# Sliding-window attention and a gated feed-forward: attention issued between the feed-forward's matmuls, with two-head block-diagonal score products and tanh for sigmoid

## The chip, the cores and the metric

The kernel runs on one core of a Trainium2 chip. The metric is the device time of one execution in microseconds (us), the median of several runs.

The core has five engines, each with its own list of instructions; the instructions of VectorE, ScalarE and GpSimd start in the order in which the kernel issues them. The engines are TensorE (PE in the profile; PEld are its weight loads, which overlap its products), VectorE (DVE), ScalarE (ACT), GpSimd (POOL) and the sync engine (SP), which here only issues transfers. "Granted clock" or PEclk is the share of TensorE's full clock that the throttle let through.

## The reference

There are 8 batches, 8 heads, 576 positions and 64 dimensions per head. Each query sees itself and the 63 positions before it. The result, laid out as 4608 tokens of 512 values, goes through a gated feed-forward with 1536 hidden values. The reference, shortened:

```python
scores = scale * np.matmul(q, k.transpose(0, 1, 3, 2))          # scale = 1/8
mask = (rel >= 0) & (rel < 64)                                  # rel = query position - key position
scores = np.where(mask, scores, -1e9)
attn = softmax(scores)                                          # written out in the original
x = (attn @ v).transpose(0, 2, 1, 3).reshape(4608, 512)
g = x @ w_gate                                                  # 512 x 1536
out = (g * (1.0 / (1.0 + np.exp(-g))) * (x @ w_val)) @ w_out    # w_out: 1536 x 512
```

## The kernel before

It works in two stages. The first goes through all 64 heads. A head's q and k are cast, transposed on TensorE, and multiplied in blocks of 64 queries by 128 keys.

```python
        for b in range(B):
            for h in range(H):
                po = (h % 2) * 64
                kc = h // 2
                qbh = q[b, h]
                kbh = k[b, h]
                vbh = v[b, h]
                # ... tiles and loads of q, k, v and of v shifted by 64 rows, on two queues ...
                q_bf = nat.tile([P, 5, D], BF16, name="q_bf", tag="q_bf")
                k_bf = nat.tile([P, 5, D], BF16, name="k_bf", tag="k_bf")
                nc.vector.tensor_copy(q_bf[:, 0:4, :], q_nat[:, 0:4, :])
                nc.vector.tensor_copy(q_bf[0:64, 4, :], q_nat[0:64, 4, :])
                nc.vector.tensor_copy(k_bf[:, 0:4, :], k_nat[:, 0:4, :])
                nc.vector.tensor_copy(k_bf[0:64, 4, :], k_nat[0:64, 4, :])
                qT = tp_pool.tile([64, S], BF16, name="qT", tag="qT")
                kT = tp_pool.tile([64, S], BF16, name="kT", tag="kT")
                tpq = psB.tile([64, 640], BF16, name="tpq", tag="tpq")
                tpk = psB.tile([64, 640], BF16, name="tpk", tag="tpk")
                for c in range(4):
                    nc.tensor.transpose(tpq[:, 128 * c:128 * c + 128], q_bf[:, c, :], identb[:])
                    nc.tensor.transpose(tpk[:, 128 * c:128 * c + 128], k_bf[:, c, :], identb[:])
                nc.tensor.transpose(tpq[:, 512:576], q_bf[0:64, 4, :], identb[0:64, 0:64])
                nc.tensor.transpose(tpk[:, 512:576], k_bf[0:64, 4, :], identb[0:64, 0:64])
                nc.scalar.copy(qT[:, :], tpq[:, 0:576])
                nc.vector.tensor_copy(kT[:, :], tpk[:, 0:576])
                # ... casts of v and of the shifted v, with a column of ones beside each ...
                groups = [list(range(8)), [8]]
                for gi, blocks in enumerate(groups):
                    nb = len(blocks)
                    mask_t = mask_first if (gi == 0) else mask_reg
                    S_ps = psA.tile([P, 8, 64], FP32, name="S_ps", tag="S_ps")
                    for mu, i in enumerate(blocks):
                        k0 = 0 if i == 0 else 64 * (i - 1)
                        nc.tensor.matmul(
                            S_ps[:, mu, :],
                            kT[:, k0:k0 + 128],
                            qT[:, 64 * i:64 * i + 64],
                        )
                    E = grp.tile([P, 8, 64], BF16, name="E", tag="E")
                    nc.scalar.activation(
                        E[:, 0:nb, :], S_ps[:, 0:nb, :], AF.Exp, bias=0.0, scale=SCALE
                    )
                    nc.vector.tensor_mul(E[:, 0:nb, :], E[:, 0:nb, :], mask_t[:, 0:nb, :])

                    ntiles = 2 if nb == 8 else 1
                    OU = []
                    for tt in range(ntiles):
                        OU.append(psA.tile([64, 4, 65], FP32, name="OU", tag="OU"))
                    for mu, i in enumerate(blocks):
                        tt = mu // 4
                        jj = mu % 4
                        if i == 0:
                            vv = v_aug[:, 0, :]
                        elif i % 2 == 1:
                            vv = v_aug[:, (i - 1) // 2, :]
                        else:
                            vv = vs_aug[:, (i - 2) // 2, :]
                        nc.tensor.matmul(OU[tt][:, jj, :], E[:, mu, :], vv)
                    R = grp.tile([64, 8], FP32, name="R", tag="R")
                    for tt in range(ntiles):
                        nbt = min(4, nb - 4 * tt)
                        nc.vector.reciprocal(R[:, 4 * tt:4 * tt + nbt], OU[tt][:, 0:nbt, 64])
                    Dm = grp.tile([64, 8, 64], BF16, name="Dm", tag="Dm")
                    nc.vector.tensor_mul(
                        Dm[:, 0:nb, :],
                        ident8[:, 0:nb, :],
                        R[:, 0:nb].to_broadcast((64, nb, 64)),
                    )
                    OU_sb = grp.tile([64, 8, 64], BF16, name="OU_sb", tag="OU_sb")
                    for tt in range(ntiles):
                        nbt = min(4, nb - 4 * tt)
                        nc.vector.tensor_copy(
                            OU_sb[:, 4 * tt:4 * tt + nbt, :], OU[tt][:, 0:nbt, 0:64]
                        )
                    XT = psA.tile([P, 8, 64], FP32, name="XT", tag="XT")
                    for mu, i in enumerate(blocks):
                        nc.tensor.matmul(
                            XT[po:po + 64, mu, :],
                            OU_sb[:, mu, :],
                            Dm[:, mu, :],
                        )
                    # ... copied into xT by ScalarE ...
```

The second stage goes through nine tiles of 512 tokens. `fps` has two PSUM banks for each of `g_ps` and `v_ps`, `fops` has one for `o_ps`.

```python
            hT = fsb.tile([P, 12, 512], BF16, name="hT", tag="hT")
            for m in range(12):
                g_ps = fps.tile([P, 512], FP32, name="g_ps", tag="g_ps")
                v_ps = fps.tile([P, 512], FP32, name="v_ps", tag="v_ps")
                for kk in range(4):
                    nc.tensor.matmul(
                        g_ps[:], wg[:, kk, 128 * m:128 * m + 128],
                        xT[:, kk, tok0:tok0 + 512],
                        start=(kk == 0), stop=(kk == 3),
                    )
                for kk in range(4):
                    nc.tensor.matmul(
                        v_ps[:], wv[:, kk, 128 * m:128 * m + 128],
                        xT[:, kk, tok0:tok0 + 512],
                        start=(kk == 0), stop=(kk == 3),
                    )
                sg = fsb.tile([P, 512], BF16, name="sg", tag="sg")
                nc.scalar.activation(sg[:], g_ps[:], AF.Sigmoid)
                tq = fsb.tile([P, 512], BF16, name="tq", tag="tq")
                nc.vector.tensor_mul(tq[:], sg[:], g_ps[:])
                nc.vector.tensor_mul(hT[:, m, :], tq[:], v_ps[:])
            for sub in range(4):
                o_ps = fops.tile([P, 512], FP32, name="o_ps", tag="o_ps")
                for kk in range(12):
                    nc.tensor.matmul(
                        o_ps[:],
                        hT[:, kk, 128 * sub:128 * sub + 128],
                        wo[:, kk, :],
                        start=(kk == 0), stop=(kk == 11),
                    )
                os_ = ostage.tile([P, 512], FP32, name="os_", tag="os_")
                nc.scalar.copy(os_[:], o_ps[:])
                nc.sync.dma_start(out[tok0 + 128 * sub:tok0 + 128 * sub + 128, :], os_[:])
```

The softmax here doesn't subtract the row's maximum and nothing guards it: scores larger than these inputs give would overflow.

## Time and profile before

| | |
|---|---|
| time | 605.42 us, median of 3 runs (604.98 to 605.86) |
| start: loads of weights, TensorE idle | 23 us |
| attention | 23 to about 315 us, about 4.5 us per head |
| feed-forward | 315 us to the end, 31.1 us per tile |

The top of the profile's page gives the span, each engine's busy time with its share and number of instructions, and then the span in 40 equal slices of 15 us, where a digit is the busy share of a slice in tenths.

```profile
span 602.7 us, 10344 instructions
...
PE 517.5 (86%) x3638; PEld 306.0 (51%) x3664; DVE 406.2 (67%) x1439; ACT 218.1 (36%) x466; POOL 3.9 (1%) x12
...
PE   0068888888888888888869999999999999999996
...
DVE  1578898898989889898966455554546463637270
...
```

Counted from 1, VectorE is at 8 or 9 tenths in slices 4 to 20 and TensorE is at 9 in slices 22 to 39. The two stages have two different limits, and the average shares (86% and 67%) describe neither. The view by windows shows it for one stretch inside each stage. Its columns are the window, its length, then busy time and number of instructions for PE, PEld, DVE, ACT and POOL, the granted clock, the DMA share and GB/s.

```profile
...
40.00:300.00 260.00, 220.29 (x2208) 166.44 (x2205) 229.52 (x1130) 121.96 (x300) 0.00 (x0) 1.00 0.57 128
320.00:590.00 270.00, 268.02 (x1224) 121.83 (x1248) 147.49 (x215) 82.77 (x140) 0.00 (x0) 1.00 0.09 32
...
```

TensorE's 220 us of "busy" time in the first window says little: its many small products are drawn overlapping (nine score products of one group span 0.66 us at 121.58 us, while the mean of one is 237 ns). The feed-forward can be read better from distances: equal projections of two tiles lie 31.08 us apart (341.11 to 372.19 us), and a tile has 144 matmuls, so one takes 0.216 us. Nine tiles need at least 280 us of TensorE. The chain that ended last says the same. It is followed back from the last instruction, and its shares are of the whole span.

```profile
...
PE 46%; ACT 0%; issue 0%; ACTq 0%
PE v_ps L221 16%; PE g_ps L215 15%; PE o_ps L234 15%; ACT os__8291 L241 0%; ACT os__8323 L241 0%; ACT os__8307 L241 0%; ACT os__8339 L241 0%; ACTq L241 0%
...
```

The costliest groups of instructions are shown with busy time, the mean time of one in ns, and the idle time before them with what ended it.

```profile
...
L229 DVE TENSOR_TENSOR tq<-sg,g_ps 128x512 bf16<-128x512 bf16 x108 | 74.2, 687 | 81.5 <-ACT sg L227 81.5
L215 PE MATMUL g_ps<-xT,wg 128*128 128x512 bf16 x422 | 110.2, 381 | 1.4 <-ACT xT L196 0.7
...
L234 PE MATMUL o_ps<-wo,hT 128*128 128x512 bf16 x424 | 98.5, 379 | 2.4 <-ACT os__8291 L241 0.7
...
L184 DVE CAST OU_sb<-OU 64x256 bf16<-64x256 f32 (+1 forms) x192 | 63.1, 329 | 0.0
...
```

The groups with shapes kept apart: first come two kinds of weight loads, then the reciprocal at two sizes.

```profile
...
L215 PEld LDWEIGHTS <-wg 128*128 128x128 bf16 x432 | 42.3, 98 | 52.0 <-issue 1.5
...
L126 PEld LDWEIGHTS <-k_bf 128*64 128x64 bf16 x256 | 27.4, 163 | 33.0 <-DVE k_bf L118 29.3 <-issue 0.9
...
L174 DVE RECIPROCAL R<-OU 64x4 f32<-64x4 f32 x128 | 22.1, 173 | 9.2 <-PE OU L170 1.7
...
L174 DVE RECIPROCAL R<-OU 64x1 f32<-64x1 f32 x64 | 9.7, 151 | 2.0
...
```

A weight load of 128 rows and 128 columns takes 98 ns and one of 128 rows and 64 columns 163 ns. The Trainium skill, page "TensorE: Matmul & The Clock Gate", section "Weight-path perf modes", says that the fast weight load is on when there are 128 weights of a type other than FP32; this trace agrees. The reciprocal of one element per partition takes 151 ns and of four 173 ns: the slope is about 7 ns per element.

### The profile page before, as it was taken

How to read it: one execution, taken by the hardware profiler on the slowest of the kernel's cores; microseconds unless marked ns; L12 is line 12 of the kernel's file. 1: busy time of each engine (PE TensorE's matmuls, PEld its weight loads, DVE VectorE, ACT ScalarE, POOL GpSimd, SP SyncE). 2: the span in 40 equal slices, each digit the busy share in tenths (PEclk: the TensorE clock that was granted, in tenths of full speed). 3: DMA queues.
4: the chain of work that ended last, by engine and by line, in shares of the span. 5: the costliest groups of instructions: out<-in, count | busy, mean ns of one | idle time of the engine just before them, and what ended most of it. 6: DMA issues, size and time to landing. Idle time of an engine off the chain costs nothing. (4 is left out here: it accounts for less than half of the span.)

```text
span 602.7 us, 10344 instructions
## 1 busy us (share of the span) xinstructions
PE 517.5 (86%) x3638; PEld 306.0 (51%) x3664; DVE 406.2 (67%) x1439; ACT 218.1 (36%) x466; POOL 3.9 (1%) x12
## 2 busy tenths in 40 slices
PE   0068888888888888888869999999999999999996
PEld 0046666666666666666654444444444444444442
DVE  1578898898989889898966455554546463637270
ACT  0044444444444444444434232333233232323331
POOL 2000000000000000000000000000000000000000
PEclk9999999999999999999999999999999999999999
DMA  8955565555656555665510000101010101010101
GB/s 345 344 125 118 124 140 130 125 122 132 136 117 139 131 129 119 136 138 117 130 28 1 35 36 29 41 18 53 18 52 18 52 4 67 2 71 0 71 0 70
DMA packets 153251, 55.20 MB, mean 92 GB/s; under 512 B 146032, under 2 KB 146032, under 8 KB 153200
## 3 DMA queue, kind: packets, MB, share of 16 engines
q1 hardware_dynamic: 79968, 33.57, 20.2%
q10 hardware_dynamic: 73232, 20.98, 14.5%
q8 instruction: 28, 0.46, 0.3%
q14 instruction: 23, 0.19, 0.1%
HBM read 45.09 MB, written 9.44 MB: 90 GB/s over the span
## 5 line engine op out<-in xcount | busy, mean ns | idle before, releaser
L229 DVE TENSOR_TENSOR tq<-sg,g_ps 128x512 bf16<-128x512 bf16 x108 | 74.2, 687 | 81.5 <-ACT sg L227 81.5
L215 PE MATMUL g_ps<-xT,wg 128*128 128x512 bf16 x422 | 110.2, 381 | 1.4 <-ACT xT L196 0.7
L221 PE MATMUL v_ps<-xT,wv 128*128 128x512 bf16 x424 | 110.5, 381 | 0.5
L230 DVE TENSOR_TENSOR hT<-tq,v_ps 128x512 bf16<-128x512 bf16 x108 | 74.1, 687 | 43.6 <-PE v_ps L221 34.2
L227 ACT ACTIVATE sg<-g_ps 128x512 bf16<-128x512 f32 x108 | 64.5, 597 | 106.2 <-PE g_ps L215 101.4
L234 PE MATMUL o_ps<-wo,hT 128*128 128x512 bf16 x424 | 98.5, 379 | 2.4 <-ACT os__8291 L241 0.7
L152 ACT ACTIVATE E<-S_ps 128x512 bf16<-128x512 f32 (+1 forms) x128 | 46.7, 408 | 76.9 <-PE S_ps L146 61.3
L234 PEld LDWEIGHTS <-hT 128*128 128x128 bf16 x432 | 42.2, 98 | 53.5 <-issue 2.9
L215 PEld LDWEIGHTS <-wg 128*128 128x128 bf16 x432 | 42.3, 98 | 52.0 <-issue 1.5
L221 PEld LDWEIGHTS <-wv 128*128 128x128 bf16 x432 | 42.4, 98 | 51.7 <-issue 1.1
L189 PE MATMUL XT<-Dm,OU_sb 64*64 64x64 bf16 x576 | 55.1, 240 | 14.5 <-DVE Dm L176 14.4
L126 PE MATMUL tpk<-identb,k_bf 128*64 128x128 bf16 x256 | 41.4, 313 | 30.2 <-DVE k_bf L118 25.5
L184 DVE CAST OU_sb<-OU 64x256 bf16<-64x256 f32 (+1 forms) x192 | 63.1, 329 | 0.0
L196 ACT CAST xT<-XT 64x512 bf16<-64x512 f32 (+1 forms) x128 | 44.1, 393 | 48.2 <-PE XT L189 46.9
L170 PEld LDWEIGHTS <-E 128*64 128x64 bf16 x576 | 41.0, 151 | 30.8 <-DVE E L155 23.1
L176 DVE TENSOR_TENSOR Dm<-ident_76,R 64x512 bf16<-64x512 bf16 (+1 forms) x128 | 56.2, 439 | 0.0
L170 PE MATMUL OU<-v_aug,E 128*64 128x65 bf16 x320 | 41.5, 248 | 15.1 <-DVE E L155 12.6
L189 PEld LDWEIGHTS <-OU_sb 64*64 64x64 bf16 x576 | 41.7, 144 | 24.5 <-DVE Dm L176 15.9
L146 PE MATMUL S_ps<-qT,kT 64*128 64x64 bf16 x576 | 42.4, 237 | 12.7 <-DVE kT L130 10.9
L129 ACT COPY qT<-tpq 64x576 bf16<-64x576 bf16 x64 | 40.3, 630 | 28.1 <-PE tpq L127 21.1
L170 PE MATMUL OU<-vs_aug,E 128*64 128x65 bf16 x256 | 46.6, 249 | 0.7 <-DVE OU_sb L184 0.6
L125 PE MATMUL tpq<-identb,q_bf 128*64 128x128 bf16 x256 | 41.9, 311 | 4.1 <-DVE q_bf L116 2.8
(76 smaller groups left out, 375.5 us busy)
## 6 DMA issues: line engine op xcount, KB each, us to landing
k_nat<-in_k_dram ACTq DMA_DIRECT2D x64, 128.0 KB, 2.8
vs_nat<-in_v_dram ACTq DMA_DIRECT2D x64, 128.0 KB, 2.6
q_nat<-in_q_dram SPq DMA_DIRECT2D x64, 128.0 KB, 2.6
v_nat<-in_v_dram SPq DMA_DIRECT2D x64, 128.0 KB, 2.8
wv_f<-in_moe_w_val_dram ACTq DMA_DIRECT2D x1, 3072.0 KB, 18.0
wg_f<-in_moe_w_gate_dram SPq DMA_DIRECT2D x1, 3072.0 KB, 17.0
wo_f<-in_moe_w_out_dram SPq DMA_DIRECT2D x1, 3072.0 KB, 27.2
k_nat<-in_k_dram ACTq DMA_DIRECT2D x64, 16.0 KB, 2.5
```

The lines of the kernel that those rows point to most:

```text
L152: nc.scalar.activation(E[:, 0:nb, :], S_ps[:, 0:nb, :], AF.Exp, bias=0.0, scale=SCALE)
L170: nc.tensor.matmul(OU[tt][:, jj, :], E[:, mu, :], vv)
L176: nc.vector.tensor_mul(Dm[:, 0:nb, :], ident8[:, 0:nb, :], R[:, 0:nb].to_broadcast((64, nb, 64)),)
L184: nc.vector.tensor_copy(OU_sb[:, 4 * tt:4 * tt + nbt, :], OU[tt][:, 0:nbt, 0:64])
L189: nc.tensor.matmul(XT[po:po + 64, mu, :], OU_sb[:, mu, :], Dm[:, mu, :],)
L196: nc.scalar.copy(xT[po:po + 64, kc, t0:t0 + 64 * nb], XT[po:po + 64, 0:nb, :],)
L215: nc.tensor.matmul(g_ps[:], wg[:, kk, 128 * m:128 * m + 128], xT[:, kk, tok0:tok0 + 512], start=(kk == 0), stop=(kk == 3),)
L221: nc.tensor.matmul(v_ps[:], wv[:, kk, 128 * m:128 * m + 128], xT[:, kk, tok0:tok0 + 512], start=(kk == 0), stop=(kk == 3),)
L227: nc.scalar.activation(sg[:], g_ps[:], AF.Sigmoid)
L229: nc.vector.tensor_mul(tq[:], sg[:], g_ps[:])
L230: nc.vector.tensor_mul(hT[:, m, :], tq[:], v_ps[:])
L234: nc.tensor.matmul(o_ps[:], hT[:, kk, 128 * sub:128 * sub + 128], wo[:, kk, :], start=(kk == 0), stop=(kk == 11),)
```

## The change

The intent is to keep TensorE on the feed-forward while the other engines prepare the attention of later tiles. The work of attention is cut into 36 units: one tile of 512 tokens and two heads each. Unit by unit it is issued between matmuls of the feed-forward of an earlier tile, in an order fixed by hand. Scores are keys by queries, as before. What is new is that the values, and not the scores, are the weights of the second product: its result comes out as head dimensions by queries, as the feed-forward needs it, so the products with `Dm`, which turned it round before, are not needed. Two heads share one product, with keys in block-diagonal weights (`kbd`) of full 128 columns; values likewise (`vbd`). The softmax sums are made by a product with a block of ones (`bones`), which leaves each sum already spread over 64 partitions, so one 128x512 reciprocal and one multiply normalize a unit. Sigmoid becomes tanh, `g * sigmoid(g) = 0.5 * g * (1 + tanh(g/2))`, with the 0.5 in `wo`. The casts of q, k and v and the masks move to GpSimd, and all transfers go on one queue.

The attention functions, new:

```diff
+    def transposes(u):
+        t, p = divmod(u, 4)
+        q_b, k_b = ready.pop(u)
+        tp = ps_a.tile([P, 2, 512], BF16, name="tp", tag="a")
+        for i, x in enumerate((q_b, k_b)):
+            for c in range(4):
+                nc.tensor.transpose(tp[:, i, P * c:P * c + P], x[:, c, :], identb[:])
+        qT = att.tile([P, 512], BF16, name="qT", tag="qT")
+        nc.scalar.copy(qT[:], tp[:, 0, :])
+        kb = kbd[t % 2]
+        kt = tp[:, 1, :].rearrange("r (j x) -> r j x", x=64)
+        nc.vector.tensor_copy(kb[0:64, p, :, 0:64], kt[0:64])
+        nc.vector.tensor_copy(kb[64:128, p, :, 64:128], kt[64:128])
+        queries[u] = qT
+
+    weights = {}
+
+    def scores(u):
+        t, p = divmod(u, 4)
+        qT = queries.pop(u)
+        E = att.tile([P, 8, 2, 64], BF16, name="E", tag="E")
+        Ef = E[:].rearrange("r m c x -> r (m c x)")
+        for h in range(2):
+            s_ps = ps_a.tile([P, 512], FP32, name="s_ps", tag="a")
+            lo = 0
+            if u < 4 and h == 0:
+                lo = 64
+            else:
+                j = 4 * h - 1
+                kb = kbd[t % 2][:, p, j, :] if j > 0 else kbd[(t - 1) % 2][:, p, 7, :]
+                nc.tensor.matmul(s_ps[:, 0:64], kb, qT[:, 256 * h:256 * h + 64])
+            for i in range(4):
+                n = P if i < 3 else 64
+                j = 4 * h + i
+                nc.tensor.matmul(
+                    s_ps[:, 64 + P * i:64 + P * i + n],
+                    kbd[t % 2][:, p, j, :],
+                    qT[:, 64 * j:64 * j + n],
+                )
+            nc.scalar.activation(
+                Ef[:, 512 * h + lo:512 * h + 512], s_ps[:, lo:512], AF.Exp, scale=0.125
+            )
+            nc.gpsimd.tensor_mul(
+                Ef[:, 512 * h + lo:512 * h + 512],
+                Ef[:, 512 * h + lo:512 * h + 512],
+                mask[:].rearrange("r m c x -> r (m c x)")[:, lo:512],
+            )
+            if t < 8 and t // 4 == h:
+                nc.gpsimd.memset(E[:, t, 0, :], 0.0)
+        weights[u] = E
+
+    xT = {}
+
+    def products(u):
+        t, p = divmod(u, 4)
+        E = weights.pop(u)
+        Ef = E[:].rearrange("r m c x -> r (m c x)")
+        if p == 0:
+            xT[t] = xpool.tile([P, 4, 512], BF16, name="xT", tag="xT")
+        o_ps = ps_a.tile([P, 512], FP32, name="ao_ps", tag="a")
+        first = True
+        for j in range(-1, 8):
+            if j < 0 and t == 0:
+                continue
+            vb = vbd[t % 2][:, p, j, :] if j >= 0 else vbd[(t - 1) % 2][:, p, 7, :]
+            lo, hi = max(0, 64 * j), min(512, 64 * j + P)
+            e0 = 64 * (2 * j + 1) if j >= 0 else 0
+            nc.tensor.matmul(
+                o_ps[:, lo:hi], vb, Ef[:, e0:e0 + hi - lo],
+                start=first, stop=(j == 7), skip_group_check=True,
+            )
+            first = False
+        d_ps = ps_a.tile([P, 512], FP32, name="ad_ps", tag="a")
+        for c in range(2):
+            nc.tensor.matmul(d_ps[:], bones[:], E[:, :, c, :], start=(c == 0), stop=(c == 1))
+        r = att.tile([P, 512], FP32, name="r", tag="r")
+        nc.vector.reciprocal(r[:], d_ps[:])
+        nc.vector.tensor_mul(xT[t][:, p, :], o_ps[:], r[:])
```

The gate, with the old lines in front:

```diff
-                nc.scalar.activation(sg[:], g_ps[:], AF.Sigmoid)
-                tq = fsb.tile([P, 512], BF16, name="tq", tag="tq")
-                nc.vector.tensor_mul(tq[:], sg[:], g_ps[:])
-                nc.vector.tensor_mul(hT[:, m, :], tq[:], v_ps[:])
+        th = fsb.tile([P, 512], FP32, name="th", tag="th")
+        nc.scalar.activation(th[:], g_ps[:], AF.Tanh, scale=0.5)
+        sg = fsb.tile([P, 512], FP32, name="sg", tag="sg")
+        nc.vector.scalar_tensor_tensor(sg[:], th[:], 1.0, g_ps[:], ALU.add, ALU.mult)
+        nc.vector.tensor_mul(hT[t][:, m, :], sg[:], v_ps[:])
```

And the order of the middle units, from the fifth (`w` = 4) on. A unit of time is a quarter of a feed-forward tile; it carries the products of unit w+4 and the transposes and scores of unit w+5:

```diff
+        gate_value(t, 3 * s)
+        if w + 4 < NU:
+            products(w + 4)
+        gate_value(t, 3 * s + 1)
+        if w + 5 < NU:
+            transposes(w + 5)
+        project(t - 1, s, ps_o, "o")
+        if w + 8 < NU:
+            load(w + 8)
+        if w + 6 < NU:
+            casts(w + 6)
+        if w + 5 < NU:
+            scores(w + 5)
+        gate_value(t, 3 * s + 2)
```

Left out here: loads, casts, the four units before the first feed-forward, and the first four units, which also cast the weights.

## The prediction

> **What bounds it now.** Two stages follow each other. In the busy table over 40 slices VectorE is at 80-90% up to about 315 us. That attention stage is bound by VectorE: 64 heads in about 290 us, 4.5 us each (casts, masks, copies, Dm). Loading takes the first 23 us: TensorE is idle. From 315 us the chain of waits is TensorE alone, 46% of the span. There one 512-token tile takes 31.1 us between equal projections, 144 matmuls at 0.216 us: TensorE's floor for the feed-forward, 280 us for nine tiles.
>
> **What changes.** Attention (36 units: 512 tokens, two heads) is issued between feed-forward matmuls, so VectorE's 290 us no longer stands in front of TensorE's 280. Casts and masks go to GpSimd; the Dm products, the v copy shifted by 64 and its loads go.
>
> TensorE, per unit (estimates from trace durations): 24 gate/value matmuls 5.2 us, 12 projection matmuls 2.6; 8 transposes at the 0.107 us spacing of today's, 0.86; scores and value products 17 to 18 at about 0.06, 1.1; two 512-wide denominators 0.43. Sum 10.2 us; 36 units: 367 us.
>
> VectorE, per unit: three times two 128x512 operations with PSUM (0.69 each, 0.62 from start to start): 3.8 us; two kT copies 0.7; the final multiply 0.62; and the new cost: the reciprocal is now 128x512. Today's 64x1 takes 151 ns and 64x4 173 ns, that is 7.3 ns per element; the Trainium skill, "VectorE: DVE Perf Modes" (walkthrough of the pipeline), says that reciprocal is an iterative divide with a repeat count of 8, which agrees. Estimate: 3.9 to 4.4 us per unit. Sum 9.2 us: below TensorE, yet not hidden, because of the order on both engines.
>
> **Critical path.** After the products of unit w+4, VectorE does reciprocal (4.2), multiply (0.6), the next gate's two operations (1.25), then kT copies (0.7). TensorE meanwhile has 5.2 us of work (gate 1.73, transposes 0.86, projection 2.6), then needs those kT copies for the scores. It waits about 2 us per unit. Loop: denominators 1.0, leftover gate on VectorE 0.35, 6.75 as above, latency 0.2, scores 0.6, two gates 3.46: 12.4 us. ScalarE (7 operations of 0.6 us, 4.2) is not limiting. Tanh for sigmoid gives nothing but one table load (1.3 us).
>
> Sum: prologue (loads, GpSimd casts and masks, four units with no feed-forward; reciprocals in series) 47 us; first four units, bound by VectorE with weight casts, 48; 28 units at 12.4: 347; last four without attention 31; last four projections and output 13. **About 485 us**, range 445 to 525. Faster by over 2%: 0.96; within 2%: 0.02; slower: 0.02.
>
> **What would show it.** Right: reciprocal group near 36 x 4.2 = 150 us, the costliest on VectorE; TensorE waits for the kT copies before scores, near 2 us each; units 12 to 13 us apart; no second table load; first gate matmul at 40 to 50 us. Wrong: reciprocal near 0.7 us: then TensorE bounds, 10.3 us per unit, about 415 us.
>
> **What would make it wrong.** GpSimd: two masks per unit lie between exp and the next products. From the skill's "GPSIMD Engine Reference" (section 3), a two-input operation costs about 2.2 ns per element; 1.1 to 1.3 us each just fits (estimate); no trace here shows it. If they take 2 us, units take 13.5 us. Load issues on one queue (up to 20 per unit, about 0.45 us each) could fall behind.

## The result and the profile after

The changed kernel takes 471.2 us (median of 4 runs, 470.18 to 472.11) against 605.64 us for the kernel before in the same rounds. The ratio is 0.7777, with a 95% interval of 0.7762 to 0.7792. Ratios here are taken from the fast runs of both kernels on one chip and are not quite the ratio of the medians.

The same two parts of the page, of the kernel after; a slice is now 11.7 us:

```profile
span 468.9 us, 6826 instructions
...
PE 367.7 (78%) x2332; PEld 189.3 (40%) x2332; DVE 338.8 (72%) x380; ACT 145.2 (31%) x253; POOL 176.9 (38%) x258
...
PE   1453866738888888888888888888888888889996
...
DVE  7188798777777777777777777777777777776540
...
PEclk9975897879999999999999999999999999999999
...
```

The two stages are gone: TensorE is at 8 and VectorE at 7 from slice 10 to 36, and neither is at 9. The first nine slices are something else: TensorE low in most of them and its granted clock between 5 and 9. By windows (columns as before), the first four units and the 28 middle ones:

```profile
...
45.00:103.00 58.00, 38.16 (x229) 19.99 (x229) 48.41 (x53) 15.04 (x27) 22.94 (x29) 0.82 0.66 184
103.00:423.00 320.00, 271.38 (x1799) 140.38 (x1797) 242.12 (x276) 109.97 (x193) 126.95 (x184) 1.00 0.33 83
...
```

In the middle window TensorE's instructions cover 271 us of 320 and VectorE's 242. No engine is full. The chain that ended last shows how the two alternate:

```profile
...
DVE 52%; PE 35%; ACT 4%; SPq 3%; issue 2%; POOL 2%; DMA 1%; DVEq 0%; POOLq 0%; ACTq 0%
DVE r L217 24%; PE g_ps L229 14%; PE v_ps L229 9%; DVE hT L237 9%; DVE sg L236 8%; PE o_ps L242 6%; DVE xT L218 5%; PE s_ps L175 4%; ACT th L234 3%; SPq L88 2%; POOL E L183 2%; DVE kbd_93 L153 1%; DVE kbd_94 L153 1%; DVE kbd_93 L152 1%; PE ad_ps L215 1%
...
```

The largest share is VectorE's reciprocal, and the groups of the page show its mean and the wait that matters:

```profile
...
L236 DVE SCALAR_TENSOR_TENSOR sg<-th,g_ps 128x512 f32<-128x512 f32 x108 | 73.9, 684 | 86.5 <-ACT th L234 86.4
L217 DVE RECIPROCAL r<-ad_ps 128x512 f32<-128x512 f32 x36 | 120.7, 3353 | 5.0 <-PE ad_ps L215 5.0
...
L242 PE MATMUL o_ps<-wo,hT 128*128 128x512 bf16 x432 | 98.6, 379 | 0.0
...
L175 PE MATMUL s_ps<-qT,kbd_93 128*128 128x128 bf16 (+1 forms) x160 | 14.0, 232 | 33.0 <-DVE kbd_93 L153 31.6
...
```

Scores (`s_ps`) cost 14.0 us of busy time in this group and 33 us of idle time before it, ended by VectorE's second copy into `kbd`; the group of the other `kbd` buffer has another 29 us on the page. The timeline of one middle unit shows the whole loop. Its columns are the start, the duration, the engine, the line, the instruction, and in brackets the idle time before it and what ended it.

```profile
...
255.34 0.58 PE L208 MATMUL ao_ps<-E,vbd_96 128*128 128x128 bf16 x8
...
255.76 0.60 PE L215 MATMUL ad_ps<-E,bones 128*128 128x512 bf16 x2
...
256.67 3.35 DVE L217 RECIPROCAL r<-ad_ps 128x512 f32<-128x512 f32 x1
...
260.06 0.69 DVE L218 TENSOR_TENSOR xT<-ao_ps,r 128x512 bf16<-128x512 f32 x1
260.67 0.68 DVE L236 SCALAR_TENSOR_TENSOR sg<-th,g_ps 128x512 f32<-128x512 f32 x1
...
261.45 0.69 DVE L237 TENSOR_TENSOR hT<-sg,v_ps 128x512 bf16<-128x512 f32 x1
262.05 0.41 DVE L152 COPY kbd_94<-tp 64x512 bf16<-64x512 bf16 x1
262.47 0.43 DVE L153 COPY kbd_94<-tp 64x512 bf16<-64x512 bf16 x1
...
262.96 0.37 PE L175 MATMUL s_ps<-qT,kbd_94 128*128 128x128 bf16 x4 [1.81 <-DVE kbd_94 L153]
...
263.39 1.03 PE L229 MATMUL g_ps<-xT,wg 128*128 128x512 bf16 x4
...
266.87 0.58 PE L208 MATMUL ao_ps<-E,vbd_96 128*128 128x128 bf16 x8
...
```

From 255.34 to 266.87 us, products of one unit to products of the next, is 11.53 us, and from the fifth unit to the end of the middle every unit takes 11.5 us. Read downwards it is one chain with hardly a gap:

| step | us |
|---|---|
| products and denominators; VectorE finishes the gate before | 1.33 |
| reciprocal 128x512 | 3.39 |
| multiply into xT | 0.61 |
| two gate operations that stand next on VectorE | 1.38 |
| two copies into kbd | 0.91 |
| scores | 0.43 |
| two gates on TensorE, then the next products | 3.48 |
| sum | 11.53 |

TensorE finished its projection about 2 us before the scores could start; the wait is 1.81 us. That is the chain that the prediction drew, with a shorter reciprocal and the other terms within 0.4 us.

### The profile page after: what moved, and what is told of

Same layout as the page of the kernel before. It is cut to its first block, busy times and chain, and to the rows that moved or that the text cites. A ratio compares the mean times of both kernels' runs of the same rounds, so it can differ in the third digit from the quotient of the medians.

```text
span 468.9 us, 6826 instructions
## 1 busy us (share of the span) xinstructions
PE 367.7 (78%) x2332; PEld 189.3 (40%) x2332; DVE 338.8 (72%) x380; ACT 145.2 (31%) x253; POOL 176.9 (38%) x258
## 4 chain that ended last, share of the span: by engine, by line
DVE 52%; PE 35%; ACT 4%; SPq 3%; issue 2%; POOL 2%; DMA 1%; DVEq 0%; POOLq 0%; ACTq 0%
DVE r L217 24%; PE g_ps L229 14%; PE v_ps L229 9%; DVE hT L237 9%; DVE sg L236 8%; PE o_ps L242 6%; DVE xT L218 5%; PE s_ps L175 4%; ACT th L234 3%; SPq L88 2%; POOL E L183 2%; DVE kbd_93 L153 1%; DVE kbd_94 L153 1%; DVE kbd_93 L152 1%; PE ad_ps L215 1%
## 5 line engine op out<-in xcount | busy, mean ns | idle before, releaser
L183 POOL TENSOR_TENSOR E<-E,mask 128x512 bf16<-128x512 bf16 (+1 forms) x72 | 84.5, 1185 | 215.4 <-ACT E L180 215.4
L236 DVE SCALAR_TENSOR_TENSOR sg<-th,g_ps 128x512 f32<-128x512 f32 x108 | 73.9, 684 | 86.5 <-ACT th L234 86.4
L217 DVE RECIPROCAL r<-ad_ps 128x512 f32<-128x512 f32 x36 | 120.7, 3353 | 5.0 <-PE ad_ps L215 5.0
L234 ACT ACTIVATE th<-g_ps 128x512 f32<-128x512 f32 x108 | 64.5, 597 | 128.4 <-PE g_ps L229 128.4
L237 DVE TENSOR_TENSOR hT<-sg,v_ps 128x512 bf16<-128x512 f32 x108 | 74.2, 687 | 11.6 <-PE v_ps L229 0.6
L180 ACT ACTIVATE E<-s_ps 128x512 bf16<-128x512 f32 (+1 forms) x72 | 39.1, 592 | 68.6 <-PE s_ps L175 68.6
L242 PEld LDWEIGHTS <-hT 128*128 128x128 bf16 x432 | 41.1, 98 | 44.6
L175 PE MATMUL s_ps<-qT,kbd_93 128*128 128x128 bf16 (+1 forms) x160 | 14.0, 232 | 33.0 <-DVE kbd_93 L153 31.6
L149 ACT COPY qT<-tp 128x512 bf16<-128x512 bf16 x36 | 21.1, 586 | 45.6 <-PE tp L147 45.6
L175 PE MATMUL s_ps<-qT,kbd_94 128*128 128x128 bf16 (+1 forms) x128 | 10.3, 224 | 29.2 <-DVE kbd_94 L153 29.2
L215 PE MATMUL ad_ps<-E,bones 128*128 128x512 bf16 x72 | 23.1, 405 | 5.4 <-DVE r L217 5.4
L218 DVE TENSOR_TENSOR xT<-ao_ps,r 128x512 bf16<-128x512 f32 x36 | 24.9, 692 | 1.2
L108 POOL CAST q_b<-q_f 128x512 bf16<-128x512 f32 x36 | 22.7, 630 | 6.1 <-DMA q_f<-in_q_dram 4.5
L147 PEld LDWEIGHTS <-q_b 128*128 128x128 bf16 x144 | 11.3, 102 | 26.0 <-POOL q_b L108 18.2
```

The source lines that it names most:

```text
L147: nc.tensor.transpose(tp[:, i, P * c:P * c + P], x[:, c, :], identb[:])
L175: nc.tensor.matmul(s_ps[:, 64 + P * i:64 + P * i + n], kbd[t % 2][:, p, j, :], qT[:, 64 * j:64 * j + n],)
L180: nc.scalar.activation(Ef[:, 512 * h + lo:512 * h + 512], s_ps[:, lo:512], AF.Exp, scale=0.125)
L183: nc.gpsimd.tensor_mul(Ef[:, 512 * h + lo:512 * h + 512], Ef[:, 512 * h + lo:512 * h + 512], mask[:].rearrange("r m c x -> r (m c x)")[:, ...
L215: nc.tensor.matmul(d_ps[:], bones[:], E[:, :, c, :], start=(c == 0), stop=(c == 1))
L217: nc.vector.reciprocal(r[:], d_ps[:])
```

## The experiments

All of them give correct results. Times of one call come from one chip with its own runs of the kernel before (605.6 to 605.9 us in every call). Diffs without other notice are against the changed kernel. The length of a unit is the distance between successive multiplies into xT in the timeline.

### Order within a unit (e1_order)

```diff
@@ -326,2 +326,4 @@
         gate_value(t, 3 * s)
+        if w + 5 < NU:
+            transposes(w + 5)
         if w + 4 < NU:
@@ -329,4 +331,2 @@
         gate_value(t, 3 * s + 1)
-        if w + 5 < NU:
-            transposes(w + 5)
         project(t - 1, s, ps_o, "o")
```

> Only the order inside a unit is changed, from the fifth unit on: the transposes of unit w+5 are issued before the products of unit w+4, so VectorE copies kT before it starts the reciprocal. Theory A (a chain through VectorE's order: reciprocal 3.35 us, multiply 0.6, gate 1.35, kT copies 0.8, then scores): TensorE's wait of 1.8 us before the scores vanishes, a unit falls from 11.5 to 9.6 to 9.9 us, and the time falls by 45 to 52 us, to about 422. Rival B (units are paced by the throughput of an engine, TensorE or GpSimd's masks, and the wait before the scores is only where that shows): the wait moves elsewhere, and the time falls by less than 10 us.

Measured: 431.85 us (ratio to before 0.7133, interval 0.7113 to 0.7152), 39 us less than the changed kernel. Most middle units take 9.55 us, but six take 10.4 to 13.5 us. So the chain through VectorE's order set the unit, and rival B falls. The gain is short of the forecast by 6 us, and the timeline shows why: in the long units GpSimd, which works in order, sits at a cast until a load lands, and the masks behind it come late. Those six units are 14 us longer than six of 9.55 us, which is more than the shortfall.

```profile
...
234.40 0.62 POOL L109 CAST k_b<-k_f 128x512 bf16<-128x512 f32 x1 [4.00 <-DMA k_f<-in_k_dram]
...
```

At that point the one queue issues 20 transfers for a unit, and the issues alone occupy it for 11.6 us (eight of q 4.49, eight of k 4.48, four of v 2.61).

### The reciprocal twice (e2_double_recip)

```diff
@@ -217,2 +217,3 @@
         nc.vector.reciprocal(r[:], d_ps[:])
+        nc.vector.reciprocal(r[:], d_ps[:])
         nc.vector.tensor_mul(xT[t][:, p, :], o_ps[:], r[:])
```

> The reciprocal is computed twice into the same tile (result still right). Theory A (the reciprocal lies on the loop that sets the unit's length): each middle unit grows by the whole 3.3 us, to 14.8 us, and with the first units the time grows by 105 to 120 us, to about 580. Rival C (VectorE's throughput or TensorE's sets the length, the 28% of idle time on VectorE takes some of it): VectorE's work per unit would be 8.5 + 3.3 = 11.8 us, so the unit grows by 0.3 us and the time by 10 to 30 us.

Measured: 648.97 us (one round, ratio to before 1.0711), 178 us more than the changed kernel. Units take 17.1 us, so the reciprocal is on the loop with its whole length, and rival C falls. But the growth is 5.5 us per unit where the second reciprocal takes 3.36. The rest is TensorE's clock: the time from the scores behind the wait to the gates is 0.80 us and not 0.43, and from there to the next products 5.23 us and not 3.48, together 2.1 us more. The timeline shows two waits of over 2 us with one 64-wide product between them, and then four matmuls in 1.90 us where the changed kernel has 1.03:

```profile
...
309.73 0.20 PE L171 MATMUL s_ps<-qT,kbd 128*128 128x64 bf16 x1 [2.36 <-DVE r L218]
...
312.61 0.56 PE L175 MATMUL s_ps<-qT,kbd 128*128 128x128 bf16 x4 [2.68 <-DVE kbd L153]
...
313.41 1.90 PE L230 MATMUL g_ps<-xT,wg 128*128 128x512 bf16 x4
...
```

```profile
...
250.00:300.00 50.00, 34.90 (x191) 17.07 (x190) 35.64 (x33) 11.86 (x21) 12.83 (x19) 0.80 0.23 57
...
```

The second fence is the window from 250 to 300 us: the granted clock, third from the end, is 0.80, and it is 1.00 in the changed kernel's middle. The Trainium skill, page "TensorE: Matmul & The Clock Gate", Part 1, says that an idle window of about 3.4 us brings the clock down to half. The trace agrees on the half: from 313 to 315 us, behind the waits, the granted clock is 0.50. Neither wait is 3.4 us long, but both together with the 0.20 us of work between them are 5.2 us. The 1.81 us waits of the changed kernel leave the clock at 1.00. No run here gives a sharp limit: in e3_sigmoid, below, units with the same wait of 2.68 us run at 1.00 (from 350 us) and at 0.88 (from 364 us). In this run, then, the waits cost 2.1 us per unit more than themselves.

### Sigmoid back (e3_sigmoid)

```diff
@@ -136,3 +136,3 @@
     def casts_o(s):
-        nc.vector.tensor_scalar_mul(wo[:, 3 * s:3 * s + 3, :], raw.pop((2, s))[:], 0.5)
+        nc.vector.tensor_copy(wo[:, 3 * s:3 * s + 3, :], raw.pop((2, s))[:])
 
@@ -233,5 +233,5 @@
         th = fsb.tile([P, 512], FP32, name="th", tag="th")
-        nc.scalar.activation(th[:], g_ps[:], AF.Tanh, scale=0.5)
+        nc.scalar.activation(th[:], g_ps[:], AF.Sigmoid)
         sg = fsb.tile([P, 512], FP32, name="sg", tag="sg")
-        nc.vector.scalar_tensor_tensor(sg[:], th[:], 1.0, g_ps[:], ALU.add, ALU.mult)
+        nc.vector.tensor_mul(sg[:], th[:], g_ps[:])
         nc.vector.tensor_mul(hT[t][:, m, :], sg[:], v_ps[:])
```

> Sigmoid in place of tanh in the interleaved kernel, with the plain multiply and the plain cast of w_out. The prediction on record said that tanh for sigmoid gives nothing but one table load: then the time changes by under 3 us. Rival: in the interleaved order ScalarE alternates between exp and sigmoid, so two table loads of 1.28 us come back in each unit, some 70 in all; the one before sigmoid delays the gate and with it the reciprocal by about 0.6 us per unit, and the time grows by 15 to 40 us.

Measured: 538.4 us (ratio 0.8886, interval 0.8872 to 0.89), 67 us more than with tanh. Units take 13.8 to 14 us. The two loads per unit are there:

```profile
...
312.73 1.28 ACT L180 ACT_TABLE_LOAD   x1 [3.11 <-PE s_ps L175]
...
314.02 1.08 ACT L180 ACTIVATE E<-s_ps 128x512 bf16<-128x512 f32 x2
...
315.12 1.28 ACT L234 ACT_TABLE_LOAD   x1
...
```

The load for exp waits for the scores just as the exp behind it does, so it adds 1.28 us between scores and masks. The load for sigmoid then holds up both gates that VectorE must finish before it can start the reciprocal. From the end of the scores to the start of the reciprocal the timeline has 7.1 us (312.71 to 319.83) where the changed kernel has 4.8: the loads added 2.3 us per unit, and not the forecast 0.6, because both lie on the loop. The granted clock is at 8 tenths in 23 of the 40 slices, but that is not what lengthens the units: units of the same 13.85 us are found at 1.00 and at 0.88.

### Attention first, feed-forward after (e4_sequential)

The new attention functions are kept and only the order is undone. The core of the edit, which replaces the interleaved loops:

```python
for u in range(NU):                  # transposes, scores, products of neighbouring units overlap
    transposes(u + 2); scores(u + 1); products(u)     # where they exist
    # ... weight casts in u = 0..7, load(u + 6), casts(u + 3) ...
for t in range(NT):
    for m in range(12):
        gate_value(t, m)
    for s in range(4):
        project(t, s, ps_o, "o")
```

`xpool` grows from 3 to 9 buffers; `stage` shrinks from 4 to 3 and `fsb` from 3 to 2 to make room.

> The new attention without interleaving: all 36 units first, then the nine feed-forward tiles (a pool deeper for x, two pools shallower for lack of space). Theory A says that new attention alone needs 4.7 us of VectorE and 4.8 us of GpSimd per unit, 5 to 6.5 us with its waits: 36 units 180 to 235 us, first weights and loads 12, feed-forward 281, end 4: 475 to 530 us, so interleaving is worth at most 60 us of the 134 gained and most of the gain is the smaller attention. Rival D (interleaving is where the gain comes from, and attention itself is as long as before, about 290 us): 580 us or more.

Measured: 648.37 us (ratio 1.0704, interval 1.0685 to 1.0724). Rival D's 580 us or more is met, and my theory's second half fell: the new attention alone is not shorter than the old (the first gate starts at 338 us, where the old feed-forward began at about 315). Units take 6.6 to 13 us; the long ones come where the loads of the tiles with the most transfers are due, and the chain that ended last gives 20% of the span to the transfer queue.

### Fewer transfers (e5_merged_loads), and both together (e6_order_merged)

```diff
@@ -86,7 +86,13 @@
                         m, r = left // P * P, P
-                    for a in range(2):
+                    if m == r:
                         nc.sync.dma_start(
-                            dst[o % P:o % P + r, o // P:o // P + max(1, m // P), a, :],
-                            src[b, 2 * p + a, s:s + m].rearrange("(c r) d -> r c d", r=r),
+                            dst[o % P:o % P + r, o // P, :, :],
+                            src[b, 2 * p:2 * p + 2, s:s + m].rearrange("a r d -> r a d"),
                         )
+                    else:
+                        for a in range(2):
+                            nc.sync.dma_start(
+                                dst[o % P:o % P + r, o // P:o // P + m // P, a, :],
+                                src[b, 2 * p + a, s:s + m].rearrange("(c r) d -> r c d", r=r),
+                            )
                     o, s, left = o + m, s + m, left - m
```

> Only the loads of the changed kernel are altered: pieces of q and k that are one block of rows are loaded for both heads by one transfer, 432 transfers on the one queue and not 528; a unit of tiles 3 and 5 has 14 and not 20. Theory A (middle units are set by the chain through VectorE, loads come early enough there): units stay at 11.5 us, the time falls by less than 4 us. Rival (the load issues on one queue set the units): several units shorten, the time falls by 10 us or more.

Measured: 471.48 us (ratio 0.7784, interval 0.7769 to 0.7799; the changed kernel had 0.7777). No middle unit changes. The load issues do not matter while the chain is longer.

The next run has this edit and that of e1_order.

> Reordered units and merged loads together. With the order alone, most middle units took 9.55 us, but six took 10.4 to 13.5 us, where casts on GpSimd waited for loads. If the load issues are the second limit behind the chain: all middle units at 9.5 to 9.7 us and about 417 us, 12 to 16 us below the order alone, although the merging alone gains under 4 us. If not: 428 us or more.

Measured: 417.86 us (ratio 0.6898, interval 0.6884 to 0.6913), 14 us below the order alone. Every middle unit takes 9.5 to 9.6 us. An edit worth nothing by itself is worth 14 us behind the other. One unit of it, with the two copies into kbd now ahead of the reciprocal:

```profile
...
260.81 0.60 PE L221 MATMUL ad_ps<-E,bones 128*128 128x512 bf16 x2
...
261.70 0.43 DVE L159 COPY kbd<-tp 64x512 bf16<-64x512 bf16 x1
...
262.15 3.36 DVE L223 RECIPROCAL r<-ad_ps 128x512 f32<-128x512 f32 x1
...
265.58 0.36 PE L181 MATMUL s_ps<-qT,kbd 128*128 128x128 bf16 x4
...
```

The scores start at 265.58 us with no wait ahead of them. TensorE is busy for all 50 of the 50 us from 250 to 300: 9.55 us is its floor.

### The sequential version, loads merged (e7_seq_merged), v on another queue (e10_seq_freer), other banks (e12_seq_psum)

The first has the diff of e5_merged_loads on e4_sequential.

> The sequential version with merged loads. If its attention (650 us in all, units of 6.6 us and of 10 to 13 us) was slow because of the load issues on one queue, the long units shrink to 7 to 9 us, and the time falls by 50 to 100 us, to 550 to 600 us; still above the interleaved kernel, since 6.6 us per unit is GpSimd's and the products' chain with a cold TensorE. If it was slow for the cold clock and dependences alone: less than 20 us.

Measured: 597.71 us (ratio 0.9862, interval 0.9845 to 0.9878). Merging the issues gained 51 us, just inside the forecast. Yet the first gate starts only at 287 us. The slices of its page show what is left: TensorE half busy in the first half of the span, at a granted clock of 5 to 7 tenths after the first four slices.

```profile
...
PE   1554556445444655466898989899998989999996
...
PEclk9999555555755555557699999999999999999999
...
```

The next run frees scores of their PSUM wait and puts v on ScalarE's queue, against e7_seq_merged:

```diff
@@ -100,3 +100,3 @@
             for a in range(2):
-                nc.sync.dma_start(
+                nc.scalar.dma_start(
                     v_f[64 * a:64 * a + 64, off // 64:(off + n) // 64],
@@ -169,3 +169,3 @@
         for h in range(2):
-            s_ps = ps_a.tile([P, 512], FP32, name="s_ps", tag="a")
+            s_ps = ps_f.tile([P, 512], FP32, name="s_ps", tag="gv"[h])
             lo = 0
```

> The sequential version freed of two limits of its own: the score tiles use the PSUM banks of the feed-forward, which are idle in that stage, and v is loaded on ScalarE's queue. If those two held its attention at 6.6 to 10 us per unit (e7_seq_merged): units of 5 to 6 us, GpSimd's 4.9 being the floor, and 510 to 550 us, still above the interleaved 471. If the cold clock and the order of dependences held it: over 570 us.

Measured: 643.27 us (ratio 1.062, interval 1.0604 to 1.0636). This was a miss of my own making. ScalarE's copies of the transposed queries stood behind those issues and waited for the loads of v; the view of waits shows it in total us, number of times and longest us:

```profile
...
ACT qT L155 <- DMA v_f<-in_v_dram: 155.7, 20, 9.1
...
```

The last run leaves the loads alone, against e7_seq_merged:

```diff
@@ -149,3 +149,3 @@
         q_b, k_b = ready.pop(u)
-        tp = ps_a.tile([P, 2, 512], BF16, name="tp", tag="a")
+        tp = ps_o.tile([P, 2, 512], BF16, name="tp", tag="o")
         for i, x in enumerate((q_b, k_b)):
@@ -169,3 +169,3 @@
         for h in range(2):
-            s_ps = ps_a.tile([P, 512], FP32, name="s_ps", tag="a")
+            s_ps = ps_f.tile([P, 512], FP32, name="s_ps", tag="gv"[h])
             lo = 0
```

> The sequential version with merged loads, all loads again on the one queue, and only the PSUM banks changed: scores and transposes in the banks that the feed-forward leaves idle in that stage. The run before it moved loads to ScalarE's queue as well, and ScalarE then waited 156 us at those issues, so it told nothing of the banks. If the banks held the sequential attention (units of 6.6 to 10 us), units of 5.5 to 7.5 us and 560 to 585 us; the loads, 12 to 14 issues of half a microsecond per unit, are the next limit. If not: within 10 us of 598. In both cases the new attention run alone stays far above what interleaving reaches (471, 418 reordered).

Measured: 590.93 us (ratio 0.9776, interval 0.9741 to 0.9811), 7 us better than e7_seq_merged and so within the second alternative: the banks were a small part. Units still vary from 5.1 to 10 us, and the chain that ended last gives 27% of the span to the queue and its transfers. How fast a sequential version could be with better loads is left open. Three attempts did not bring it under 590 us, with the same functions that take 471 us interleaved.

### A combined version (e8_combined)

Against e6_order_merged:

```diff
@@ -116,4 +116,8 @@
         vb = vbd[t % 2]
-        nc.gpsimd.tensor_copy(vb[0:64, p, :, 0:64], v_f[0:64])
-        nc.gpsimd.tensor_copy(vb[64:128, p, :, 64:128], v_f[64:128])
+        if u < 4:
+            nc.scalar.copy(vb[0:64, p, :, 0:64], v_f[0:64])
+            nc.scalar.copy(vb[64:128, p, :, 64:128], v_f[64:128])
+        else:
+            nc.gpsimd.tensor_copy(vb[0:64, p, :, 0:64], v_f[0:64])
+            nc.gpsimd.tensor_copy(vb[64:128, p, :, 64:128], v_f[64:128])
         ready[u] = (q_b, k_b)
@@ -132,3 +136,3 @@
         for i, dst in enumerate((wg, wv)):
-            nc.vector.tensor_copy(dst[:, :, 384 * s:384 * s + 384], raw.pop((i, s))[:])
+            nc.scalar.copy(dst[:, :, 384 * s:384 * s + 384], raw.pop((i, s))[:])
 
@@ -142,3 +146,3 @@
     def casts_o(s):
-        nc.vector.tensor_scalar_mul(wo[:, 3 * s:3 * s + 3, :], raw.pop((2, s))[:], 0.5)
+        nc.scalar.mul(wo[:, 3 * s:3 * s + 3, :], raw.pop((2, s))[:], 0.5)
 
@@ -260,8 +264,6 @@
     load(4)
-    for i in range(2):
-        nc.vector.memset(kbd[i][:], 0.0)
     make_identity(nc, identb[:])
-    for i in range(2):
-        nc.vector.memset(vbd[i][:], 0.0)
-    casts(0)
+    nc.vector.memset(mask[:], 1.0)
+    nc.vector.memset(kbd[0][:], 0.0)
+    nc.vector.memset(vbd[0][:], 0.0)
     nc.vector.memset(bones[:], 0.0)
@@ -269,3 +271,2 @@
     nc.vector.memset(bones[64:128, 64:128], 1.0)
-    nc.vector.memset(mask[:], 1.0)
     for a in range(2):
@@ -282,2 +283,3 @@
 
+    casts(0)
     transposes(0)
@@ -286,2 +288,4 @@
     transposes(1)
+    nc.vector.memset(kbd[1][:], 0.0)
+    nc.vector.memset(vbd[1][:], 0.0)
     scores(0)
@@ -319,8 +323,10 @@
                 casts_gv(w + 1)
+            else:
+                casts_o(0)
+                casts_o(1)
             scores(w + 4)
             gate_value(t, 3 * s + 2)
-            products(w + 4)
             if w == 3:
-                for i in range(4):
-                    casts_o(i)
+                casts_o(2)
+                casts_o(3)
                 load(10)
@@ -329,2 +335,5 @@
                 casts(9)
+            products(w + 4)
+            if w == 3:
+                project(0, 0, ps_o, "o")
                 scores(8)
@@ -337,3 +346,4 @@
         gate_value(t, 3 * s + 1)
-        project(t - 1, s, ps_o, "o")
+        if w > 4:
+            project(t - 1, s, ps_o, "o")
         if w + 8 < NU:
```

> Reordered units, merged loads, and the start shortened: mask and first constants made first, v casts of the first four units and all weight casts on ScalarE, projection of the first block ahead of the gate that waits for x of tile 1. From the 417 us expected of the two together: 4 to 6 us less before the first gate, 2.6 us less VectorE work in three of the first four units, 4 to 8 us less at the fourth: about 395 to 405 us.

Measured: 404.69 us (ratio to before 0.6683, interval 0.6673 to 0.6694). It beats both kernels: against the changed kernel the ratio is 0.6683 / 0.7777 = 0.859, an estimate over two chips. The first gate matmul is at 35.6 us and not 41.1 (e6_order_merged). Behind the first multiply into xT after that, two units fall from 12.4 and 12.6 us to 11.5 and 11.3, and the next two together from 27.3 to 21.1.

```profile
...
PE 362.5 (90%) x2332; PEld 189.6 (47%) x2332; DVE 326.9 (81%) x368; ACT 162.4 (40%) x273; POOL 167.3 (41%) x250
...
PE   1554776887999999999999999999999999999996
...
```

### The doubled reciprocal off the loop (e9_order_double_recip)

The edit of e2_double_recip on e6_order_merged.

> The doubled reciprocal once more, now in the reordered kernel with merged loads (418 us). Theory A says that there the reciprocal is off the loop that sets the unit, so doubling only makes VectorE the busiest engine: 8.5 + 3.35 = 11.85 us per unit against TensorE's 9.55, so units of 11.9 to 12.3 us, and the time grows by 75 to 95 us in place of 178, to about 500 us. If the loop still held it: units of 15 us or more and 580 us or more.

Measured: 526.31 us (ratio 0.868, interval 0.8659 to 0.87), 108 us more than e6_order_merged, where the same edit cost 178 us in the changed kernel. Middle units take 12.4 us, 2.9 more, where they had grown by 5.5. VectorE is at 9 tenths in nearly every middle slice, so it is now the busiest engine, as said. The units from the tenth on grow by 75 us together, the low end of the forecast; my number was low by the 32 us that came before them, where the units (15 to 19 us) stay chained.

### Sigmoid in the combined version (e11_combined_sigmoid)

The edit of e3_sigmoid on e8_combined, with `nc.scalar.copy` for the scaled cast of `wo`.

> The combined kernel (404.7 us) with sigmoid in place of tanh. If the two table loads per unit are on the critical loop in any interleaved order, because exp waits for the scores, its load waits with it, and the masks and products follow: units of 10.5 to 12 us in place of 9.55 and the time up by 30 to 80 us. If TensorE's work hides them once VectorE's chain is gone: under 10 us.

Measured: 446.92 us (ratio 0.7388, interval 0.736 to 0.7417), 42 us more. Units alternate between 10.4 and 11.2 us. So the time is within the first forecast, but its reason is only half right. The trace has almost no wait for scores before the loads for exp (1.1 us in all, against 85 in e3_sigmoid). TensorE now waits before the scores for the reciprocal (27 us in 26 waits), which starts behind the late gates. Tanh is worth 67 us in one interleaved order and 42 in the other; whether an order exists that hides the loads is not shown.

## Why the prediction was right or wrong

It said 485 us with 445 to 525 us; measured were 471.2 us. The mechanism was right and sizes were off in both directions. That the total is only 14 us off is in part luck: the first four units were put 9 us too low and the middle ones 26 us too high. The spans in the trace, from the first gate matmuls and the gates of the fifth, 33rd and last units:

| part | predicted us | measured us |
|---|---|---|
| up to the end of the first gate's g matmuls | 47 | 46 |
| first four units | 48 | 57 |
| 28 middle units | 347 (12.4 each) | 321 (11.5 each) |
| last four without attention | 31 | 31 |
| last projections and output | 13 | 14 |

- **The bound before.** VectorE bound the first stage and TensorE the second. That was read from the profile; the sequential runs test what follows from it: with the same new functions, order, with the buffer counts that it needs, makes 598 us into 471 (e7_seq_merged against e5_merged_loads), or 591 with other banks (e12_seq_psum). In the runs made, then, nearly the whole gain over 605 us is overlap; the restructured attention run by itself gained 15 us at most. Two things are not shown: how fast a better sequential version would be, and what interleaving the old attention would give. VectorE's work in the old kernel, 406 us, is by itself less than 471, so that rival stays open.
- **The loop.** "VectorE does reciprocal (4.2), multiply (0.6), the next gate's two operations (1.25), then kT copies (0.7)": shown. TensorE waits 1.8 us (about 2 predicted); moving the copies ahead of the reciprocal takes the wait away (e1_order), and lengthening the reciprocal lengthens the unit (e2_double_recip).
- **The mis-sized term of the loop.** "Estimate: 3.9 to 4.4 us per unit": the reciprocal took 3.35 us and not the 4.2 in the loop, which is nearly the whole 0.9 us by which a middle unit was shorter. The slope between one and four elements, 7.3 ns, does not hold at 512: (3353 - 151) / 511 = 6.3 ns. The estimate also let the repeat count of 8 in the skill's page speak for the upper end.
- **TensorE's work.** "Sum 10.2 us" per unit: the reordered kernel shows 9.55. The transposes were sized with today's 0.107 us spacing; eight now take 0.45 us and not 0.86. That did not show in the changed kernel, which waited anyway.
- **The first units.** "first four units, bound by VectorE with weight casts, 48": bound so, 48.4 us of VectorE in that 58 us window, but a weight cast took 0.95 to 1.91 us, where the cast before, 3.36 us for four times the size, gives an estimate of 0.84. The longest, 1.80 to 1.91 us, are those that start while a GpSimd mask runs, and five of the six masks beside them took 1.62 to 1.93 us where they take 1.15 in the middle units. With the weight casts on ScalarE (e8_combined), every full-size mask of the first units took 1.15. The clock of 0.82 there was not reckoned with.
- **The step that was wrong, though no term of the sum.** "Tanh for sigmoid gives nothing but one table load (1.3 us)". It costs 67 us to put sigmoid back (e3_sigmoid), and 42 us in the combined version. The step counted table loads in the old order, where exp and sigmoid each have a stage of their own. The change's own order alternates them, and tanh, which shares exp's table, is what makes that order affordable. The Trainium skill, page "ScalarE: Activation LUTs", section "Table sets: the hidden batching unit", lists tanh beside exp; the profile after agrees with one table load in the whole run.
- **The named risks.** GpSimd's masks took 1.19 us each on average, inside the 1.1 to 1.3 estimated, and just fit. Load issues on one queue did not fall behind in the changed kernel (e5_merged_loads), but did as soon as the chain was shortened (e1_order).

## What to carry to other kernels

When stages with different limits are interleaved, the sum of work per engine is only a floor; walk once around the loop of the hand-made order, because one long instruction in a strict queue, with something short and urgent behind it, can set the period although no engine is full. Moving the short instruction ahead of the long one was worth 39 us here, and a second limit, transfer issues, showed itself only then. Before interleaving two functions on ScalarE, see that they share a table.

## What the Trainium skill lacked or had wrong

- "VectorE: DVE Perf Modes" (walkthrough of the pipeline) describes reciprocal as an iterative divide with a repeat count of 8 and gives no time. Measured: 3353 ns for 128x512 f32 out of PSUM, against 692 ns for a multiply of that size; 6.3 ns per element by slope, which at the 0.96 GHz that the page states is 6.0 cycles (estimate), so the repeat count can't be read as cycles per element.
- "DMA: Bandwidth & Descriptors" (section "Issuing engines are not separate DMA queues") says of the sequencer's time to initiate transfers that it "is usually small relative to the DMA itself". Here an issue occupied the queue for about 0.56 us (eight in 4.49 us, e1_order) and a transfer of q, k or v landed 2.0 to 3.1 us after its issue, so for one transfer the sentence holds. What it leaves out is that issues on one queue add up: 20 per unit were 11.6 us, more than a unit of 9.55, and merging some of them gained 14 us once the loop allowed it.
- "ScalarE: Activation LUTs" (section "What ACT_TABLE_LOAD costs") gives 1283 ns for the load, which the trace shows exactly, plus about 1380 ns of drain, which it does not: in e3_sigmoid exp ends at 315.10 us, the next load runs from 315.12 to 316.40 and sigmoid starts at 316.42. The page doesn't say that the load waits together with the instruction that needs it, which put it on the critical loop (the 32 loads for exp began only behind 85 us of waits for the scores).
- "GPSIMD Engine Reference" (section 3.1) has 4497 ns for a two-input operation of 2048 fp32 elements, 2.2 ns each. The mask multiply of 512 bf16 elements took 1.15 us in the middle units, 2.3 ns each, so bf16 brought nothing here; no figure for that is on the page. The page does say that GpSimd contends with VectorE for SBUF, when VectorE runs in a 2-port mode or has two inputs in SBUF; the profile after fits this and adds a size: the mask of 1.15 us takes 1.62 us beside VectorE's weight casts, and such a cast takes up to 1.91 us where the shortest took 0.95.

```profile
...
52.40 1.62 POOL L183 TENSOR_TENSOR E<-E,mask 128x512 bf16<-128x512 bf16 x1 [6.87 <-ACT E L180]
...
52.93 1.91 DVE L127 CAST wv<-w_f 128x1536 bf16<-128x1536 f32 x1
...
```
